# A windowed-attention and routed-MoE kernel: score matmuls in tiles of 32 columns, both masks of a unit together, and loads paced by matmuls

## The chip, the cores and the metric

The kernel runs on one core of a Trainium2 chip. The core has a matmul engine (TensorE; PE in the profile, its weight loads PEld), a vector engine (VectorE, DVE), a scalar engine (ScalarE, ACT), a third engine for elementwise work and gathers (GpSimd, POOL) and a sequencer (SyncE, SP) that here only issues DMAs. Matmul results go to PSUM, which has eight banks of 128 partitions by 512 fp32 numbers; everything else lives in SBUF. The metric is the time of one execution in device microseconds, as the median of several runs.

## The reference

The computation has two stages. The first is attention for 8 batches of 8 heads with head size 64, over 512 local tokens, each of which sees the local tokens at a distance of at most 32 and all 32 global tokens; the 32 global tokens see everything. The second sends each token through one expert of 8 (two matmuls with a relu between them), where the expert is chosen by a scan over the sequence that keeps the previous choice unless a gate is under one half.

```python
k_all, v_all = concat([k_g, k_l]), concat([v_g, v_l])
out_g = softmax(q_g @ k_all.T / 8) @ v_all
s_ll  = where(abs(i - j) <= 32, q_l @ k_l.T / 8, -1e9)
out_l = softmax(concat([q_l @ k_g.T / 8, s_ll])) @ v_all
x = concat([out_g, out_l]) as (batch, 544, 512)
logits = x @ w_gate; local_gate = sigmoid(x @ w_local)
e[s] = argmax(logits[s]) if s == 0 or local_gate[s] < 0.5 else e[s-1]
out[s] = softmax(logits[s])[e] * (relu(x[s] @ w1[e]) @ w2[e])
```

The inputs are random; `q_g` is eight times larger than the rest.

## The kernel before

**Units and steps.** Attention runs over 48 units in an order written out by hand in `Attn.run`: for each batch `l0 l1 g0 l2 g1 l3`. An `l` unit holds the local queries of one pair of heads, a `g` unit the global queries of two pairs. Step s starts unit s and finishes unit s-2, so that every engine always has two units in hand. Each engine takes its instructions in the order in which the program issues them, and semaphores hold an instruction until its inputs are there and its output buffer is free.

**An `l` unit.** `prep` has POOL copy the queries into `qbd` (a block-diagonal layout: 128 contraction rows, 16 windows, 2 heads, 32 queries, where the other head's 64 rows are zero) and the keys into `kx`, one unit ahead and with two buffers of each (L191, L193). For each half of the unit, `l_s` takes a PSUM bank, writes the additive mask into the window's first and last 32 columns with one bf16 matmul against an identity (L238), and adds the scores with eight matmuls, one for each window: 64 columns of weights (both heads of a window) against 128 keys (L243). The contraction spans 128 rows. `l_max` has DVE take the row maximum and the difference (L248, L250), and `l_exp` has ACT take the exponential (L254). Two steps later `l_t` transposes the probabilities (L260, eight 128 by 128 transposes) and ACT copies them out (L262), and `l_av` multiplies them with the values: 16 matmuls a half, with 32 columns of weights each, which write the four groups of 32 PSUM partitions in turn (L276); DVE then normalizes into `xa` (L279 to L284).

**A `g` unit.** `g_s` makes four matmuls with 64 columns of weights (L296); its exponentials, transposes (L328) and value matmuls (L339, 32 columns) follow in the same way.

**Pieces between.** `f1` (L352), `f1g` (L359), `f2` (L367), `f2g` (L375) and `f3` (L385, L388) turn a finished batch into router logits. `fpiece` puts at most one of them between the first score half and the first value half of a step, and one before the second value half. `drip` feeds small DVE, ACT and POOL instructions of the routing between the DVE instructions of the attention; `f4` stores a batch's `xa` (1 MB), `xg` and `gx` to memory.

**Loads.** SP issues every load in program order. A load waits only for its buffer to be free: four buffers `raw` for queries and keys, five `v` for values. At an `l` step the program issues the queries and keys of the pair two ahead and the values of the pair one ahead (1,040 KB in one DMA), so that SP runs ahead of the other engines until the buffers are full.

**After the attention.** The rest of the kernel is expert matmuls in fp32r (L1256, L1267), whose weights SP loads into the same `raw` buffers and others.

In the profile an fp32 matmul is two records, a transpose and a bf16 matmul one. So a score half is 16 records of L243 behind one of L238 for the mask, a value half 32 records of L276.

## Time and profile before

| what | value |
|---|---|
| median of three runs | 690.67 us (690.36 to 690.69) |
| the profiled execution's own time | 694.06 us |
| span of its instructions | 692.3 us |
| attention, to the first expert matmul | about 232 us of the span |
| PE busy in the whole span | 97% |
| DVE, ACT, POOL busy | 62%, 50%, 30% |
| DMA queues, mean rate | 219 GB/s |

The profiler takes one execution. A row of the timeline gives the start in microseconds, the time to the end of the last of the records that it merges, the engine, the line of the program, the operation with the tiles that it writes and reads, rows by columns of the weights, the shape, and the number of records; what stands in brackets is idle time of the engine before it and what ended it. Matmuls overlap, so the time that a group takes is read from its start to the next group's start, not from its own length.

### The profile page before, as it was taken

What the parts mean: (1) busy time and instruction counts of PE and PEld (TensorE: products, weight loads), DVE (VectorE), ACT (ScalarE), POOL (GpSimd) and SP (SyncE); (2) the same over time, 40 slices, a digit from 0 to 9 for tenths busy, and PEclk for the clock granted to TensorE, in tenths of its full rate; (3) what the DMA queues carried; (4) which work ended last, traced back from release to release, by engine and by line L of the source; (5) the groups of instructions that cost most, each with busy time, mean ns of one, the idle gap of its engine ahead of it and who ended that gap; (6) DMA issues with size and microseconds to landing.
All of it is one profiled execution on the core that took longest, in us unless ns stands there. A gap on an engine that the chain in (4) does not pass through costs nothing.

```text
span 692.3 us, 18408 instructions
## 1 busy us (share of the span) xinstructions
PE 670.5 (97%) x7253; PEld 561.1 (81%) x7253; DVE 426.2 (62%) x1050; ACT 342.9 (50%) x614; POOL 207.7 (30%) x342
## 2 busy tenths in 40 slices
PE   9999999999989899998998999999999999999995
PEld 7777777777767787897887988889898889888994
DVE  7878677688887777995517535335354516255572
ACT  4555556555455674653326625344444325255553
POOL 7634334343674301033013303040404020133023
PEclk9999999999999999999999999999999999999999
DMA  8956957866856497777418647337475417265673
GB/s 318 405 220 233 346 193 309 310 248 231 299 196 273 147 356 243 260 243 245 174 60 308 232 149 239 102 117 235 145 225 191 140 61 231 66 222 193 212 270 103
DMA packets 43011, 151.44 MB, mean 219 GB/s; under 512 B 7965, under 2 KB 9245, under 8 KB 38688
## 3 DMA queue, kind: packets, MB, share of 16 engines
q1 hardware_dynamic: 35536, 126.92, 51.6%
q0 software_dynamic: 6960, 21.90, 9.5%
q8 instruction: 77, 1.26, 0.7%
q14 instruction: 150, 1.23, 0.6%
q10 hardware_dynamic: 288, 0.13, 0.1%
HBM read 130.55 MB, written 19.69 MB: 217 GB/s over the span
## 4 chain that ended last, share of the span: by engine, by line
PE 60%; DVE 3%; issue 1%; ACT 0%; POOL 0%; POOLq 0%; DVEq 0%; ACTq 0%
PE ps L1267 29%; PE ps L1256 27%; PE ps L1210 3%; DVE wq L1165 1%; DVE wp L1165 1%; PE ps L1004 0%; PE ps L1379 0%; DVE xl L1165 0%; DVE xT L994 0%; POOL xa L1196 0%; DVE xT L996 0%; POOLq L1427 0%; DVE wp L1213 0%; PE ps L276 0%; DVE wq L1371 0%
## 5 line engine op out<-in xcount | busy, mean ns | idle before, releaser
L1273 POOL DMA_INDIRECT out_dram<-y,tk x39 | 40.4, 1036 | 317.6 <-ACT y L1272 246.3
L1267 PE MATMUL ps<-wp,wq 128*128 128x512 f32 x504 | 128.4, 402 | 1.0 <-ACT wq L1370 1.0
L1267 PEld LDWEIGHTS ps<-wp,wq 128*128 128x128 f32 x504 | 93.5, 190 | 21.1 <-ACT wq L1370 1.2
L1256 PE MATMUL ps<-wp,wp 128*128 128x256 f32 (+5 forms) x672 | 109.3, 322 | 0.2 <-issue 0.2
L1256 PEld LDWEIGHTS ps<-wp,wp 128*128 128x128 f32 x672 | 103.6, 188 | 5.3 <-issue 0.4
L1259 DVE SCALAR_TENSOR_TENSOR wq<-ps,wq 128x256 fp32r<-128x256 f32 (+5 forms) x80 | 41.7, 525 | 72.8 <-ACT wq L1258 62.6
L1213 DVE TENSOR_TENSOR wp<-ps,wp 128x512 fp32r<-128x512 f32 x40 | 27.5, 691 | 78.9 <-ACT wp L1212 78.8
L1258 ACT ACTIVATE wq<-ps 128x256 fp32r<-128x256 f32 (+5 forms) x80 | 37.3, 468 | 78.3 <-PE ps L1256 68.8
L191 POOL TENSOR_SCALAR_AFFINE_SELECT qbd<-raw 64x512 f32<-64x512 f32 x62 | 44.4, 716 | 103.3 <-PE ps L243 85.5
L243 PE MATMUL ps<-kx,qbd 128*64 128x128 f32 x1024 | 71.3, 280 | 0.2 <-issue 0.2
L1272 ACT ACTIVATE y<-ps,pp 128x512 f32<-128x512 f32 x39 | 26.9, 690 | 77.7 <-PE ps L1267 71.1
L243 PEld LDWEIGHTS ps<-kx,qbd 128*64 128x64 f32 x1024 | 55.1, 137 | 12.2 <-issue 7.8
L248 DVE TENSOR_REDUCE mx<-ps 128x4 f32<-128x512 f32 x64 | 43.9, 687 | 29.9 <-PE ps L243 29.9
L1165 DVE TENSOR_TENSOR wp<-raw,wp 128x1024 fp32r<-128x1024 f32 x47 | 57.0, 1217 | 2.8 <-ACT wp L1155 2.8
L254 ACT ACTIVATE pe<-pe 128x512 f32<-128x512 f32 x64 | 40.7, 637 | 31.7 <-DVE pe L250 31.7
L1196 POOL DMA_INDIRECT xa<-xs,idx x42 | 50.9, 1212 | 17.1 <-issue 9.4
L1155 ACT CAST wp<-raw 128x1024 fp32r<-128x1024 f32 x49 | 50.8, 1047 | 0.8 <-ACT hh L1258 0.5
L1212 ACT CAST wp<-ps 128x512 fp32r<-128x512 f32 x40 | 23.4, 590 | 53.9 <-PE ps L1210 53.3
L250 DVE TENSOR_TENSOR pe<-ps,mx 128x512 f32<-128x512 f32 x64 | 44.0, 688 | 1.6
L276 PEld LDWEIGHTS ps<-v,pt 128*32 128x32 f32 x2048 | 33.4, 110 | 13.1 <-issue 7.3
L276 PE MATMUL ps<-v,pt 128*32 128x65 f32 x2048 | 42.8, 222 | 1.1 <-issue 0.4
L262 ACT COPY pt<-ps 128x512 f32<-128x512 f32 x64 | 34.9, 610 | 17.6 <-PE ps L260 17.6
(280 smaller groups left out, 1183.3 us busy)
## 6 DMA issues: line engine op xcount, KB each, us to landing
raw<-in_w_dram SPq DMA_DIRECT2D x78, 512.0 KB, 4.1
v<-in_vw_dram SPq DMA_DIRECT2D x32, 1040.0 KB, 9.8
raw<-in_qk_dram SPq DMA_DIRECT2D x32, 528.0 KB, 8.2
xa<-in_w_dram SPq DMA_DIRECT2D x26, 512.0 KB, 5.2
xT<-in_w_dram SPq DMA_DIRECT2D x20, 512.0 KB, 3.5
xs<-xa SPq DMA_DIRECT2D x8, 1056.0 KB, 4.9
qgb<-in_qg_dram SPq DMA_DIRECT2D x8, 128.0 KB, 3.5
xa<-xs,idx POOLq DMA_INDIRECT x42
```

Source lines behind the costliest of these rows:

```text
L191: self.nc.gpsimd.affine_select(out=out, in_=in_, pattern=pat, compare_op=ALU.is_ge, fill=0.0, base=0, channel_multiplier=0)
L243: nc.tensor.matmul(sp[64 * t2:64 * t2 + 64, t], qbd[:, w], kf[:, f:f + P], start=False, stop=True, skip_group_check=True)
L248: nc.vector.tensor_reduce(out=mx, in_=st["sp"], axis=AX.X, op=ALU.max)
L250: nc.vector.tensor_tensor(out=st["pe"][:, 4 * hb:4 * hb + 4], in0=st["sp"], in1=mx.broadcast_to([P, 4, P]), op=ALU.subtract)
L254: self.nc.scalar.activation(out=pe, in_=pe, func=AF.Exp, scale=SCALE)
L276: nc.tensor.matmul(o[32 * w4:32 * w4 + 32, g, h], pt[:, 2 * g + w4 // 2, w4 % 2, h, :], v[:, w, h * (D + 1):(h + 1) * (D + 1)], start=True ...
L1155: nc.scalar.copy(out=hi, in_=raw)
L1165: (nc.gpsimd if pool else nc.vector).tensor_tensor(out=lo, in0=raw, in1=hi.bitcast(F32), op=ALU.subtract)
L1196: self.nc.gpsimd.indirect_dma_start(out=self.xr[j] if k == "early" else self.xr4[:, j], out_offset=None, in_=src, in_offset=bass.IndirectO ...
L1256: nc.tensor.matmul(ph, a[:, dc, fs], b_[:, dc, n0:n1], start=(n == 0), stop=(n == 11))
L1259: nc.vector.scalar_tensor_tensor(out=hl[:, fc, n0:n1], in0=ph, scalar=0.0, in1=hh[:, fc, n0:n1].bitcast(F32), op0=ALU.max, op1=ALU.subtract)
L1267: nc.tensor.matmul(py, a[:, fc, js], b_[:, fs], start=(fc == 0 and k == 0), stop=(fc == 7 and k == 2))
```

## The change

- `l_s` and `g_s` issue two matmuls with 32 columns of weights (one head each) where one with 64 columns stood. The contraction stays at 128 rows, so that the number of score matmuls doubles and each has half the columns.
- A new `l_m` takes both PSUM banks of an `l` unit and writes both masks right behind the transposes at the start of the step. The second mask stood between the first value half and the second score half.
- Loads are issued by a new `feed`, once in the middle of a step and once at its end. `get` makes each of them wait for the matmul last issued in the program at that place (`gate`). Values come in two DMAs of 520 KB, and queries and keys of the next batch come at the steps k = 3 and k = 5 of a batch of six.
- The store of `xa` is two DMAs in place of one.

The order of PE around the step of an `l2` unit, before. `ps_66` and `ps_63` are the banks of its two score halves, `v_136` belongs to the value halves of unit s-2, L260 are that unit's transposes, and L367 and L385/L388 are pieces.

```order
L260 MATMUL ps_67<-idf,pe_137 128x128 x4
L260 MATMUL ps_68<-idf,pe_137 128x128 x4
L238 LDWEIGHTS idb
L238 MATMUL ps_66<-mask,idb 128x4x2x32
L243 MATMUL ps_66<-kx_146,qbd_144 64x128 x8
L367 MATMUL ps_70<-xT,wgl 32x512 x4
L276 MATMUL ps_69<-v_136,pt_142 32x65 x16
L238 LDWEIGHTS idb
L238 MATMUL ps_63<-mask,idb 128x4x2x32
L243 MATMUL ps_63<-kx_146,qbd_144 64x128 x8
L385 MATMUL ps_64<-idf,gsb 128x128 x4
L276 MATMUL ps_69<-v_136,pt_143 32x65 x16
```

The same place of PE with the change (transposes L289, masks L259, scores L272, `f2` L398, values L305, `f3` L416):

```order
L289 MATMUL ps_67<-idf,pe_137 128x128 x4
L289 MATMUL ps_68<-idf,pe_137 128x128 x4
L259 LDWEIGHTS idb
L259 MATMUL ps_66<-mask,idb 128x4x2x32
L259 LDWEIGHTS idb
L259 MATMUL ps_63<-mask,idb 128x4x2x32
L272 MATMUL ps_66<-kx_146,qbd_144 32x128 x16
L398 MATMUL ps_70<-xT,wgl 32x512 x4
L305 MATMUL ps_69<-v_136,pt_142 32x65 x16
L272 MATMUL ps_63<-kx_146,qbd_144 32x128 x16
L416 MATMUL ps_64<-idf,gsb 128x128 x4
L305 MATMUL ps_69<-v_136,pt_143 32x65 x16
```

The second mask has moved up past a score half, a piece and a value half, and the shape of the score matmuls is 32x128, 16 to a half, where it was 64x128, 8 to a half.

The order of SP's queue for the loads of the third batch, before (`raw` are queries and keys, `qgb` global queries, `v` values):

```order
L178 DMA raw_77<-in_qk_dram 128x1056
L182 DMA qgb_152<-in_qg_dram 128x256
L188 DMA v_134<-in_vw_dram 128x2080
L178 DMA raw_78<-in_qk_dram 128x1056
L188 DMA v_135<-in_vw_dram 128x2080
L178 DMA raw_79<-in_qk_dram 128x1056
L188 DMA v_136<-in_vw_dram 128x2080
```

and with the change, around the same loads, where PE's semaphore is among what each load but that of `qgb` waits for:

```order
L174 DMA v_134<-in_vw_dram 128x1040 x2
L174 DMA raw_77<-in_qk_dram 128x1056
L174 DMA qgb_152<-in_qg_dram 128x256
L174 DMA raw_78<-in_qk_dram 128x1056
L174 DMA v_135<-in_vw_dram 128x1040 x2
L174 DMA raw_79<-in_qk_dram 128x1056
L174 DMA raw_80<-in_qk_dram 128x1056
L174 DMA v_136<-in_vw_dram 128x1040 x2
```

`raw_79` and `raw_80` now stand ahead of `v_136`, and each value tile comes in two loads.

The diff, cut where a hunk only follows from another:

```diff
 
+    def get(self, out, in_):
+        d = self.nc.sync.dma_start(out, in_)
+        if self.gate is not None:
+            self.tc.add_manual_dep(d.ins, self.gate.ins.name, mybir.DependencyInfo(mybir.DependencyClass.Sync, mybir.DependencyReason.DATA), reason="pace")
+
     def load(self, b, pr):
-        nc = self.nc
         if pr == 0:
...
         t = c[("qk", pr)] = self.ld()
-        nc.sync.dma_start(t, self.qk[b, pr])
+        self.get(t, self.qk[b, pr])
 
...
         g = self.cur[b]["qg"] = self.qgb()
-        self.nc.sync.dma_start(g, self.qg[b])
-
-    def loadv(self, b, pr):
-        nc = self.nc
-        v = self.v()
-        self.cur[b]["v"].append(v)
-        nc.sync.dma_start(v.rearrange("p w c -> p (w c)"), self.vw[b, pr])
+        self.get(g, self.qg[b])
+
+    def loadv(self, b, pr, hf):
+        vs = self.cur[b]["v"]
+        if hf == 0:
+            vs.append(self.v())
+        n = NW // 2 * VW
+        self.get(vs[pr].rearrange("p w c -> p (w c)")[:, n * hf:n * hf + n], self.vw[b, pr][:, n * hf:n * hf + n])
+
+    def feed(self, s, hf):
+        b, k = divmod(s, 6)
+        if k < 3:
+            if b == 0 and k < 2 and hf == 0:
+                self.load(0, 2 + k)
+            self.loadv(b, 1 + k, hf)
+            return
+        b += 1
+        if b == B:
+            return
+        if k == 4:
+            self.loadv(b, 0, hf)
+        else:
+            self.load(b, (k - 3) + hf)
+            if (k, hf) == (3, 0):
+                self.load_g(b)
 
...
 
+    def l_m(self, st):
+        nc = self.nc
+        b, pr = st["u"]
+        if pr == 0:
+            self.cur[b]["xa"] = self.xa()
+            self.cur[b]["xg"] = self.xg()
+        st["pe"] = self.pe()
+        st["sps"] = [self.bank(self.ps_s) for _ in range(2)]
+        for hb, sp in enumerate(st["sps"]):
+            mo = sp.rearrange("p t (k c) -> p t k c", c=32)[:, :, 0::3, :]
+            nc.tensor.matmul(mo, self.cst.idb, self.mask[:, 4 * hb:4 * hb + 4], start=True, stop=False, skip_group_check=True)
+
     def l_s(self, st, hb):
         nc = self.nc
-        if hb == 0:
-            b, pr = st["u"]
-            if pr == 0:
-                self.cur[b]["xa"] = self.xa()
-                self.cur[b]["xg"] = self.xg()
-            st["pe"] = self.pe()
         qbd = st["qbd"]
         kf = st["kx"].rearrange("p m c k -> p (m c k)")
-        sp = st["sp"] = self.bank(self.ps_s)
-        mo = sp.rearrange("p t (k c) -> p t k c", c=32)[:, :, 0::3, :]
-        nc.tensor.matmul(mo, self.cst.idb, self.mask[:, 4 * hb:4 * hb + 4], start=True, stop=False, skip_group_check=True)
+        sp = st["sp"] = st["sps"][hb]
         for t in range(4):
...
                 f = 32 * (3 * (w // 2) + w % 2)
-                nc.tensor.matmul(sp[64 * t2:64 * t2 + 64, t], qbd[:, w], kf[:, f:f + P], start=False, stop=True, skip_group_check=True)
+                for h in range(2):
+                    r = 64 * t2 + 32 * h
+                    self.gate = nc.tensor.matmul(sp[r:r + 32, t], qbd[:, w, h], kf[:, f:f + P], start=False, stop=True, skip_group_check=True)
 
...
                     w = 8 * hb + 4 * g + w4
-                    nc.tensor.matmul(o[32 * w4:32 * w4 + 32, g, h], pt[:, 2 * g + w4 // 2, w4 % 2, h, :],
+                    self.gate = nc.tensor.matmul(o[32 * w4:32 * w4 + 32, g, h], pt[:, 2 * g + w4 // 2, w4 % 2, h, :],
                                      v[:, w, h * (D + 1):(h + 1) * (D + 1)], start=True, stop=True, skip_group_check=True)
...
                 k = c[("qk", pr)][:, SL:]
-                nc.tensor.matmul(sp[64 * i:64 * i + 64, 0:n1 - n0], c["qg"][:, pr], k[:, n0:n1], start=True, stop=True, skip_group_check=True)
+                for h in range(2):
+                    r = 64 * i + 32 * h
+                    self.gate = nc.tensor.matmul(sp[r:r + 32, 0:n1 - n0], c["qg"][:, pr, h], k[:, n0:n1], start=True, stop=True, skip_group_check=True)
             st["sp"].append(sp[:, 0:n1 - n0])
...
                 pr, h = 2 * pp + i // 2, i % 2
-                nc.tensor.matmul(op[32 * i:32 * i + 32, 0:D + 1], st["pt"][:, ci, 32 * i:32 * i + 32],
+                self.gate = nc.tensor.matmul(op[32 * i:32 * i + 32, 0:D + 1], st["pt"][:, ci, 32 * i:32 * i + 32],
                                  c["v"][pr][:, w, h * (D + 1):(h + 1) * (D + 1)], start=(ci == 0), stop=(ci == 5), skip_group_check=True)
...
         r0 = P * (1 + col(b))
-        nc.sync.dma_start(self.xs[r0:r0 + 4 * P].rearrange("(t p) r -> p t r", p=P), xa)
+        for t in range(0, 4, 2):
+            nc.sync.dma_start(self.xs[r0 + t * P:r0 + t * P + 2 * P].rearrange("(t p) r -> p t r", p=P), xa[:, t:t + 2])
         r0 = P * (1 + gcol(hf)) + 32 * b4
...
         self.load_g(0)
-        self.loadv(*pairs[0]["u"])
+        for hf in range(2):
+            self.loadv(0, 0, hf)
         self.cst.ident()
...
             if nl:
-                if npr + 2 < len(pairs):
-                    b, i = pairs[npr + 2]["u"]
-                    self.load(b, i)
-                    if i == 0:
-                        self.load_g(b)
-                if npr + 1 < len(pairs):
-                    self.loadv(*pairs[npr + 1]["u"])
                 npr += 1
...
             if nl:
+                self.l_m(nx)
                 self.l_s(nx, 0)
...
                 self.g_max(nx)
+            self.feed(s, 0)
             fpiece()
...
                 self.g_av(st)
+            self.feed(s, 1)
             if nl:
```

More of the change, by code (lines that the diff above doesn't have):

```diff
@@ L134, in __init__ @@
         self.npr = 0
+        self.gate = None
     def make_mask(self):
```

## Prediction

> **What bounds the kernel now.** I read the page first, then busy time by stretches of one batch each, then what PE waited for, then PE's timeline inside a step.
>
> ```profile
> PE 670.5 (97%) x7253; PEld 561.1 (81%) x7253; DVE 426.2 (62%) x1050; ACT 342.9 (50%) x614; POOL 207.7 (30%) x342
> ```
>
> ```profile
> 56.71:85.17 28.46, 28.05 (x588) 21.28 (x587) 21.75 (x77) 16.01 (x38) 11.67 (x27) 1.00 0.75 275
> 85.17:112.81 27.64, 27.64 (x589) 21.20 (x588) 20.55 (x69) 16.01 (x38) 10.46 (x23) 1.00 0.72 268
> 112.81:140.59 27.78, 27.78 (x589) 21.17 (x588) 21.14 (x73) 16.01 (x38) 11.06 (x25) 1.00 0.79 289
> ...
> 168.87:201.51 32.64, 30.83 (x615) 23.09 (x614) 27.41 (x97) 16.00 (x38) 23.24 (x46) 1.00 0.67 239
> 201.51:231.59 30.08, 29.06 (x610) 22.32 (x609) 23.21 (x77) 17.07 (x38) 12.42 (x22) 1.00 0.71 264
> ```
>
> The columns are the stretch, its length, busy time of PE, PEld, DVE, ACT and POOL, the clock, the share of the DMA engines and GB/s. A batch takes 27.7 us and PE is busy for all of it; DVE is at 74 to 76%, ACT at 58%, the DMA engines at 0.72 to 0.79. In the last two stretches, where the routing runs beside, DVE is at 84% and 77%, and PE idles 1.8 and 1.0 us.
>
> ```profile
> PE ps L276 <- issue: 0.4, 1, 0.4
> PE ps L243 <- issue: 0.2, 1, 0.2
> ```
>
> These are all of PE's waits from 28 to 160 us (engine and line, what ended the wait, us in total, times, longest): 0.6 us, none of it for a load. So attention is bound by PE. But "busy" holds something that is no streaming, and the timeline shows it:
>
> ```profile
> 107.31 1.09 PE L260 MATMUL ps<-idf,pe 128*128 128x128 f32 x8
> 108.24 0.27 PE L238 MATMUL ps<-mask,idb 128*128 128x256 bf16 x1
> 108.44 1.09 PE L243 MATMUL ps<-kx,qbd 128*64 128x128 f32 x16
> 109.46 0.67 PE L276 MATMUL ps<-v,pt 128*32 128x65 f32 x32
> 110.06 0.28 PE L238 MATMUL ps<-mask,idb 128*128 128x256 bf16 x1
> 110.27 1.09 PE L243 MATMUL ps<-kx,qbd 128*64 128x128 f32 x16
> 111.30 0.67 PE L276 MATMUL ps<-v,pt 128*32 128x65 f32 x32
> ```
>
> Start to start, a score half (128*64: 128 rows, 64 columns of weights) takes 1.02 us, a value half 0.60, a mask 0.20. Compare groups that are followed by one of the same width:
>
> ```profile
> 66.30 1.14 PE L296 MATMUL ps<-raw,qgb 128*64 128x256 f32 x8
> 67.36 0.27 PE L375 MATMUL ps<-xgT,wgg 128*32 128x32 f32 x8
> 67.45 0.64 PE L276 MATMUL ps<-v,pt 128*32 128x65 f32 x32
> ...
> 71.36 1.07 PE L367 MATMUL ps<-xT,wgl 128*32 128x512 f32 x8
> 72.24 0.64 PE L276 MATMUL ps<-v,pt 128*32 128x65 f32 x32
> ```
>
> L367 has 32 columns of weights, four matmuls side by side: 8 records of 512 columns are 2 x 512 = 1,024 column times and take 0.88 us to the next 32-column group. A score half is 16 records of 128 columns, two side by side, also 1,024 column times, and takes 1.02 to the next group, which is of another width. The difference, 0.14 us, is what a change of width costs. The value half gives the same: 32 records of 65 columns, four side by side, are 520 column times, 0.45 us at L367's pace, and it takes 0.60 before a mask: 0.15. L375, 8 records with 32 columns each, hands over to L276 in 0.09. I take 0.145 us for a change of width.
>
> **The change part by part.**
>
> *Score matmuls in 32 columns.* There are 64 score halves:
>
> ```profile
> L243 PE MATMUL ps<-kx,qbd 128*64 128x128 f32 x1024 | 71.3, 280 | 0.2 <-issue 0.2
> L238 PE MATMUL ps<-mask,idb 128*128 128x256 bf16 x64 | 17.8, 279 | 0.0
> ```
>
> Each becomes 32 records of 128 columns, four side by side: again 1,024 column times. No row has just this shape, but it lies between L276 (65 columns: 0.60 - 0.145 = 0.455 us for 32 records) and L367 (512 columns: 0.11 us a record), and both go at the same 0.86 to 0.88 ns a column time. So the arithmetic costs as before, and what is won is the width. For the records that are added the rows allow two ends: nothing, or the whole of the present 55 ns a record (0.88 / 16) if that is a price per record and not per column. L276's 14 ns a record (0.455 / 32) says that it is per column, and I take nothing.
>
> I counted neighbours in PE's order, before and with the change. Of the 64 score halves, 38 are now followed by a 32-column group (values, `f2`, or the second score half); before, each was followed by a change of width. Of the value halves, 23 were followed by a mask and are now followed by scores. Of the `g` units' scores, 8 are now followed by `f2g` or values. Against that, 7 pieces `f1` that were followed by a mask of their own width are now followed by scores. 38 + 23 + 8 - 7 = 62 changes of width fewer, at 0.145: 9.0 us. If neighbours of one width cost the wait too, it is 0; if a change of width costs the 0.17 us that PEld idles before such a group, 10.5:
>
> ```profile
> 111.30 0.50 PEld L276 LDWEIGHTS ps<-v,pt 128*32 128x32 f32 x32 [0.17 <-issue]
> ```
>
> *Both masks behind the transposes.* A mask before scores takes 0.20 us. The first of a pair is now followed by one of its own shape. The nearest row is that of expert matmuls with 256 columns and full width, in the chain that ended last:
>
> ```profile
> 638.13 11.34 PE ps L1256 x96
> ```
>
> 0.118 us each. So 32 masks cost 0.118 in place of 0.20: 2.7 us. The ends: 0, if the identity has to be loaded anew between the two and PE waits for it, and 4.6, if the whole 0.145 goes; L1256 loads new weights for every matmul, so I keep 2.7. The second bank must be free some 2 us earlier; there are four banks, an `l` unit takes two, and its predecessor but one has been read by then, since DVE takes each half up at once and has 24% to spare. Cost nothing; without that cover, PE would wait for L250, 0.69 us.
>
> Together PE has 11.7 us less to do.
>
> *Loads behind matmuls.* SP issued loads as early as buffers allowed, in bursts, and they landed late but long before use:
>
> ```profile
> v<-in_vw_dram SPq DMA_DIRECT2D x32, 1040.0 KB, 9.8
> raw<-in_qk_dram SPq DMA_DIRECT2D x32, 528.0 KB, 8.2
> ```
>
> (KB each and median us from issue to landing.) Now each waits for a matmul, one portion in a half step, 0.53 MB in 2.3 us. The tightest is the first pair of the next batch: issued behind the first score half at k = 3, copied by POOL, used by the first scores at k = 0. Before, these two were here:
>
> ```profile
> 98.65 1.09 PE L243 MATMUL ps<-kx,qbd 128*64 128x128 f32 x16
> ...
> 112.81 1.09 PE L243 MATMUL ps<-kx,qbd 128*64 128x128 f32 x16
> ```
>
> ```profile
> 111.45 1.50 POOL L191 TENSOR_SCALAR_AFFINE_SELECT qbd<-raw 64x512 f32<-64x512 f32 x2 [6.04 <-PE ps L243]
> 113.02 1.33 POOL L191 TENSOR_SCALAR_AFFINE_SELECT kx<-raw 128x128 f32<-128x128 f32 x4
> ```
>
> 14.2 us from the one to the other; less 1.0 for the matmul, 2.9 for the copies, and some 0.8 that the step shrinks, 9.5 us are left for a landing that took 8.2 with up to 3 MB in flight. With one portion in flight it will be shorter. Values are issued three steps ahead. Behind a waiting load in SP's queue stand the next loads and the stores of `xa`, `xg` and `gx`, whose buffers are needed again two batches later; and behind those stores the second half of one value tile, needed two steps later:
>
> ```profile
> 119.55 0.38 SPq L413 DMA_DIRECT2D xs<-xa  x1
> 119.98 3.60 SPq L417 DMA_DIRECT2D xs<-xg  x4
> ```
>
> They take SP 4 us of a batch, and the second DMA for `xa` adds another 0.4, under those two steps of 9 us. So the pacing costs nothing, and since PE waited for no load, it wins nothing.
>
> *Who is late next.* DVE. A half costs it 0.69 (L248) + 0.69 (L250) + 0.16 + 0.18 + 0.42 (L279 to L284) = 2.14 us:
>
> ```profile
> 109.58 0.69 DVE L248 TENSOR_REDUCE mx<-ps 128x4 f32<-128x512 f32 x1 [1.43 <-PE ps L243]
> ...
> 110.31 0.69 DVE L250 TENSOR_TENSOR pe<-ps,mx 128x512 f32<-128x512 f32 x1
> 110.92 0.15 DVE L279 TENSOR_SCALAR rs<-ps 128x4 f32<-128x4 f32 x1
> ...
> 111.10 0.18 DVE L281 RECIPROCAL rs<-rs 128x4 f32<-128x4 f32 x1
> ...
> 111.32 0.42 DVE L284 TENSOR_TENSOR xa<-ps,rs 128x256 f32<-128x256 f32 x1
> ```
>
> Over a batch its 21 us still fit into 27.7 - 1.4 = 26.3 (80%). In the two routing batches it rises to some 27.4 of 31.2 (88%) and 23.2 of 28.6 (81%), where PE waits already; I let half of their two times 1.4 us be lost, 1.4 us, and 0.4 in the first two steps, which wait for copies and not for PE. 11.7 - 1.8 = 9.9 us.
>
> The profiled execution took 694.06 us around a span of 692.3, 0.5% above the median of 690.67. 9.9 us less is 684.2 there and **680.8 us** as a median. The expert stage is the same code and starts as much earlier.
>
> **The rivals.**
>
> *B, DVE takes half.* Within a unit, two score halves now follow each other after 1.33 us (0.88 + 0.45) in place of 1.83, and DVE has 2.14 us for each. If the backlog reaches the next unit's value halves, whose two banks DVE must empty, half of PE's 11.7 us comes back as waits on L284, beside the 0.4 at the start: 685.2, up to 688. For it, such waits are there in the routing batches (PE's waits from 160 to 232 us):
>
> ```profile
> PE ps L352 <- DVE xa L284: 1.0, 2, 0.6
> PE ps L276 <- DVE xa L284: 0.4, 1, 0.4
> ```
>
> Against: pieces, transposes and `g` units let DVE catch up, and it idles 24%.
>
> *C, loads come late (the other side).* If a landing takes longer than those 9.5 us, PE waits for POOL's copies in each of 7 batches. At 11 us it costs 1.5 x 7 = 10.5 us, which eats the gain; that is the point from which the kernel is slower. At 13 us, 24.5 us: 705. For it: the medians of 8.2 and 9.8 are near. Against: they come from bursts.
>
> *D, a price per record.* The score and `g` matmuls double. If a record costs 55 ns whatever its columns, a score half takes 1.76 us: 64 x 0.88 = 56, and 690.7 + 56 - 11.7 = 735. It is slower than before from 33 ns on (0.88 + 11.7 / 64 = 1.06, over 32). L276's 14 ns speak against it. [...]
>
> *E, the waits stay.* If PE also empties itself between 32-column scores, which add to a bank, and 32-column values, only the masks gain: 688. Against it, L367 hands over in 0.88, and L339, which adds to its bank too, goes at L276's pace:
>
> ```profile
> 106.49 0.89 PE L339 MATMUL ps<-v,ptg 128*32 128x65 f32 x48
> ```
>
> (0.82 us to the transposes at 107.31, less 0.145, over 48: 14 ns a record).
>
> **How the numbers follow.** A 0.60, B 0.22, C 0.05, D 0.03, E 0.05, and 0.05 for B and E together, which ends at no change. A by itself lies between 677.5 (10.5 + 2.7 and nothing lost) and 683. The range goes from 677 to 686.5: it takes in A and most of B, 0.8 in all. A measurement of this kernel tells 0.2% (1.4 us) from no change. Faster: A, B and E, 0.87; same 0.05; slower, C and D, 0.08.
>
> **What would show it.** In the new profile a score half before a value half should take 0.86 to 0.90 us start to start, a value half before scores 0.45, the first mask 0.12, and a batch 26.3 us with PE busy throughout. Waits of PE on L284's successor say B; waits on POOL's copies, with POOL waiting for a load of `raw`, say C; score halves over 1.0 us say D if their records are spread evenly, E if the gap is at the end. What would make it wrong above all is DVE's lateness, which I priced by a share and not by a chain.

## The result and the profile after

The changed kernel takes 713.42 us (median of four runs, 712.40 to 714.97) beside 690.68 for the kernel before in the same session: a ratio of 1.033 (95% interval 1.0305 to 1.0354). It is slower, by 22.7 us, where 680.8 was forecast. The profiled span is 710.8 us. The first expert matmul starts at 249.5 us where it started at 231.6, and what follows takes 461.3 us as against 460.7: the loss lies in the attention.

The page of the changed kernel, busy time of the whole span:

```profile
PE 667.8 (94%) x8405; PEld 563.7 (79%) x8405; DVE 424.7 (60%) x1050; ACT 344.3 (48%) x614; POOL 209.2 (29%) x342
```

PE has 1,152 records more and is busy for 2.7 us less, in a span that is 18.5 us longer. The stretches of one batch each (the columns are as in the prediction: stretch, length, busy time of PE, PEld, DVE, ACT, POOL, clock, DMA share, GB/s):

```profile
30.44:57.05 26.61, 26.38 (x733) 21.16 (x732) 21.26 (x81) 16.05 (x38) 11.07 (x25) 1.00 0.82 253
57.05:91.51 34.46, 28.73 (x732) 22.28 (x731) 20.86 (x73) 16.20 (x38) 11.06 (x25) 0.90 0.73 222
91.51:125.56 34.05, 29.75 (x733) 22.64 (x732) 21.91 (x74) 16.49 (x39) 11.91 (x27) 0.90 0.73 235
125.56:156.84 31.28, 27.79 (x732) 21.79 (x731) 20.21 (x72) 16.00 (x38) 10.27 (x23) 0.95 0.78 242
156.84:188.12 31.28, 26.95 (x733) 20.80 (x732) 22.38 (x82) 16.48 (x39) 11.07 (x25) 1.00 0.79 254
```

The first of these batches takes 26.6 us: the 26.3 of the prediction came true here. From the next one on a batch takes 31 to 34, and the clock falls below 1.00. PE inside an undisturbed step (L259 masks, L272 scores, L305 values):

```profile
87.38 0.38 PE L259 MATMUL ps<-mask,idb 128*128 128x256 bf16 x2
87.69 1.08 PE L272 MATMUL ps<-kx,qbd 128*32 128x128 f32 x32
88.59 0.64 PE L305 MATMUL ps<-v,pt 128*32 128x65 f32 x32
89.05 1.06 PE L272 MATMUL ps<-kx,qbd 128*32 128x128 f32 x32
89.92 0.64 PE L305 MATMUL ps<-v,pt 128*32 128x65 f32 x32
```

A score half takes 0.90 and 0.87 us start to start, a value half before scores 0.46, the pair of masks 0.31 (0.12 + 0.20 was forecast). PE's work got shorter as foreseen. What takes the time stands in the waits from 28 to 250 us (engine and line, what ended the wait, us in total, times, longest):

```profile
DVE xa L313 <- DMA xs<-xa: 26.4, 8, 7.6
...
PE ps L398 <- DVE xa L313: 13.3, 4, 5.0
...
PE ps L383 <- DVE xa L313: 3.7, 6, 1.2
```

DVE waits for the store of `xa`, and PE for DVE. Here is the first time. SP's queue:

```profile
58.19 9.95 SPq L174 DMA_DIRECT2D v<-in_vw_dram  x5
68.23 0.90 SPq L445 DMA_DIRECT2D xs<-xa  x2
```

DVE:

```profile
64.20 0.08 DVE L800 MEMSET xa<- 128x28 f32 x1
...
69.07 0.18 DVE L310 RECIPROCAL rs<-rs 128x4 f32<-128x4 f32 x1
76.82 0.42 DVE L313 TENSOR_TENSOR xa<-ps,rs 128x256 f32<-128x256 f32 x1 [7.57 <-DMA xs<-xa]
```

PE:

```profile
71.18 1.08 PE L272 MATMUL ps<-kx,qbd 128*32 128x128 f32 x32
77.30 1.94 PE L398 MATMUL ps<-xT,wgl 128*32 128x512 f32 x8 [5.04 <-DVE xa L313]
79.01 1.09 PE L305 MATMUL ps<-v,pt 128*32 128x65 f32 x32
```

The tile of batch 0 is complete at 64.3 us, its store is issued at 68.2, since the fifth value load ahead of it in SP's queue waits for a matmul, and lands at 76.8. There are two `xa` buffers, and the first value half of batch 2 has to be written into this one at 69.3. The kernel before, at the same place (SP, then DVE):

```profile
63.46 0.38 SPq L413 DMA_DIRECT2D xs<-xa  x1
```

```profile
63.35 0.08 DVE L771 MEMSET xa<- 128x28 f32 x1
...
68.63 0.42 DVE L284 TENSOR_TENSOR xa<-ps,rs 128x256 f32<-128x256 f32 x1
```

It issued the store as soon as the tile was complete, and 5.2 us later, little more than the median landing time of 4.9 us, the buffer was written again. That reuse had no time to spare, and I had not looked at it. With the change the store is late twice over: at the four stalls it is issued 3.9 to 4.6 us after the tile is complete, and its first half then takes another 5.2 to 8.5 us to land.

The stall costs twice. Windows of the changed kernel behind it:

```profile
75.00:76.00 1.00, 0.00 (x0) 0.00 (x0) 0.00 (x0) 0.00 (x0) 0.00 (x0) 0.50 0.31 86
...
80.00:81.00 1.00, 1.00 (x28) 0.92 (x24) 0.76 (x3) 0.63 (x1) 0.00 (x0) 0.50 0.77 283
81.00:82.00 1.00, 1.00 (x20) 0.72 (x12) 0.31 (x2) 0.00 (x0) 0.32 (x1) 0.89 0.03 10
```

The granted clock is 0.50 for 6.8 us from the middle of the stall, and L398 above takes 1.71 us to the next group where 0.88 was its pace. The attention has three such stretches (6.8, 6.8 and 3.4 us), the kernel before none. The first begins at 74.4 us, when PE has stood for 2.1 us of a stall of 5.0; the other two begin at 108.5 and 142.7 us, inside stalls of 2.7 and 3.3 us. Two more stalls, of 2.6 us up to 21.5 and of 2.3 us up to 174.4, have none.

So that kernels can be compared, each is split in the same way: the end of the attention, less all waits of PE up to there, less half of the time that PE worked at half clock. The rest is what PE had to do.

```
kernel            end    PE waits  of these:            half   rest
                  of     in all    for     behind xa    clock
                  att.             nothing              loss
before            231.6     5.1      0.8      1.4        0.0   226.5
after             249.5    26.7      4.5     17.3        6.4   216.4
```

The rest fell by 10.1 us; waits rose by 21.6 and half clock by 6.4. "Nothing" are waits that the profile names "issue": nothing that it shows was missing.

### The profile page after: what moved, and what is told of

Read it like the earlier page. It is cut to its first block, busy times and chain, and to the rows that moved or that the text cites. A ratio compares the mean times of both kernels' runs of the same rounds, so it can differ in the third digit from the quotient of the medians.

```text
span 710.8 us, 20840 instructions
## 1 busy us (share of the span) xinstructions
PE 667.8 (94%) x8405; PEld 563.7 (79%) x8405; DVE 424.7 (60%) x1050; ACT 344.3 (48%) x614; POOL 209.2 (29%) x342
## 4 chain that ended last, share of the span: by engine, by line
PE 54%; DVE 6%; issue 1%; ACT 1%; POOL 0%; POOLq 0%; DVEq 0%; ACTq 0%
PE ps L1296 26%; PE ps L1285 24%; PE ps L1239 2%; DVE wp L1194 2%; DVE wq L1194 1%; DVE hl L1288 1%; PE ps L1408 1%; DVE xT L1023 0%; DVE xT L1025 0%; POOL xa L1225 0%; DVE o L939 0%; DVE xl L1242 0%; PE ps L1033 0%; POOLq L1456 0%; DVE wp L1242 0%
## 5 line engine op out<-in xcount | busy, mean ns | idle before, releaser
L272 PE MATMUL ps<-kx,qbd 128*32 128x128 f32 x2048 | 70.6, 280 | 0.2 <-POOL kx L214 0.2
L272 PEld LDWEIGHTS ps<-kx,qbd 128*32 128x32 f32 x2048 | 54.7, 112 | 8.7 <-issue 6.0
L1225 POOL DMA_INDIRECT xa<-xs,idx x42 | 51.5, 1226 | 17.3 <-issue 9.7
L305 PE MATMUL ps<-v,pt 128*32 128x65 f32 x2048 | 44.8, 226 | 5.7 <-issue 3.8
L305 PEld LDWEIGHTS ps<-v,pt 128*32 128x32 f32 x2048 | 36.6, 113 | 17.0 <-issue 11.6
L214 POOL TENSOR_SCALAR_AFFINE_SELECT kx<-raw 128x384 f32<-128x384 f32 (+3 forms) x127 | 42.7, 369 | 2.7 <-DMA raw<-in_qk_dram 0.6
```

The source lines that it names most:

```text
L214: self.nc.gpsimd.affine_select(out=out, in_=in_, pattern=pat, compare_op=ALU.is_ge, fill=0.0, base=0, channel_multiplier=0)
L272: self.gate = nc.tensor.matmul(sp[r:r + 32, t], qbd[:, w, h], kf[:, f:f + P], start=False, stop=True, skip_group_check=True)
L305: self.gate = nc.tensor.matmul(o[32 * w4:32 * w4 + 32, g, h], pt[:, 2 * g + w4 // 2, w4 % 2, h, :], v[:, w, h * (D + 1):(h + 1) * (D + 1)] ...
L1225: self.nc.gpsimd.indirect_dma_start(out=self.xr[j] if k == "early" else self.xr4[:, j], out_offset=None, in_=src, in_offset=bass.IndirectO ...
```

## The experiments

The expectations name theories by letters. S: the store of `xa` is late behind gated loads. T: the narrow matmuls themselves cost more. H: the halved portions and the new order of the loads cost. Later I: PE gets its instructions late. A, B, C and D are the prediction's; Q, W, N and R are said where they come. Runs of one session are compared with the kernel before on the same chip.

**e1_tiles: the matmuls alone.** The kernel before with 32-column scores and both masks together; loads and stores as before.

```diff
+                for h in range(2):
+                    r = 64 * t2 + 32 * h
+                    nc.tensor.matmul(sp[r:r + 32, t], qbd[:, w, h], kf[:, f:f + P], ...)
```

> The score tiles of 32 columns and the two masks together, with the loads and stores as they were before. Theory S (a store of xa stands behind a load that waits for a matmul, DVE waits for the store, PE for DVE): nothing of that is here, and PE has 11.7 us less to do, so 679 to 684 us. Rival T (the new tiles themselves cost time): above 691.

**e2_paced: the loads alone.** The changed kernel with the old `l_s` and `g_s` (64 columns, second mask in its old place).

> The loads behind matmuls in half portions and the store in two, with PE's work as before. Theory S: all of the loss is here, 713 and the 11.7 us that PE has more to do, some 720 to 726 us. Rival T: at most 700.

**e3_no_gate: no load waits for a matmul.** The changed kernel, with its order of loads, portions and split store.

```diff
-        if self.gate is not None:
+        if False:
             self.tc.add_manual_dep(...)
```

> The changed kernel without the wait of a load for a matmul; order, halves and the two-part store stay. Theory S: the store gets past the loads as soon as their buffers are free, and the time is that of the tiles alone, 679 to 686 us. Rival H (half portions and the new order are what makes the stores late): above 700.

**e4_store_act: stores from ACT's queue.** In `f4` of the changed kernel every `nc.sync.dma_start` becomes `nc.scalar.dma_start`.

> The changed kernel with the stores of xa, xg and gx issued by ACT in place of SP, so that no load stands ahead of them; every load still waits for its matmul. Theory S: the 26 us in which DVE waited for stores go to under 5, and the time to 684 to 692 us (the first steps stay late by 2 to 3 us). Rival C (loads for POOL's copies come late): above 704.

Measured, in one session (before 692.2):

```
kernel         us     ratio (95%)             end of att.  for nothing  behind xa  half clock  rest
e1_tiles      706.7   1.019 (1.012 to 1.026)     244.7        17.2         2.9        3.3      217.4
e2_paced      715.2   1.033 (1.028 to 1.038)     252.8         0.3        14.7        9.9      223.8
e3_no_gate    709.3   1.022 (1.017 to 1.028)     249.4        19.3         3.0        4.9      218.8
e4_store_act  738.0   1.067 (1.061 to 1.072)     262.5         1.9         2.7       13.2      216.4
```

The matmuls (with the masks) and the loads each lose by themselves. e2 shows the stall without any change of PE's work, though its time lies below the 720 to 726 expected; its waits of DVE, then of PE:

```profile
DVE xa L307 <- DMA xs<-xa: 27.1, 8, 6.2
```

```profile
PE ps L390 <- DVE xa L307: 13.6, 4, 3.9
```

and in e3, with the gate gone, the wait is gone with it:

```profile
DVE xa L313 <- DMA xs<-xa: 0.9, 2, 0.6
```

So the gate, and not the portions, makes the store late: that much of S is shown. Whether the store is late by its place in the queue or by what is in flight while it lands, e3 can't tell; e4 and e8 can. With the portions and the new order e3 is about where e1 is, so H is out, though the time is above 700 as H had it. But e1 and e3 are slow too, and e1 has none of the new loads. PE's work is short in it (217.4), so T is out as well, and PE waits 17.2 us for nothing that the profile shows:

```profile
PE ps L249 <- issue: 5.7, 3, 2.6
PE ps L304 <- issue: 3.6, 3, 2.2
PE ps L347 <- issue: 2.9, 4, 1.1
```

These waits stand inside or between groups whose inputs are there (e1's timeline; L336 transposes, L304 the scores of a `g` unit), while the DMA engines are full (e1's windows):

```profile
51.55 0.88 PE L336 MATMUL ps<-idf,pg 128*128 128x128 f32 x6
54.61 1.12 PE L304 MATMUL ps<-raw,qgb 128*32 128x256 f32 x16 [2.18 <-issue]
```

```profile
50.00:52.00 2.00, 2.00 (x58) 1.54 (x50) 1.86 (x6) 0.43 (x1) 1.43 (x2) 1.00 0.97 386
52.00:54.00 2.00, 0.43 (x4) 0.30 (x3) 1.21 (x7) 1.39 (x3) 1.33 (x4) 1.00 1.02 411
```

That is a second mechanism, which none of my theories had. e4 missed: issuing the seven stores of a batch keeps ACT's queue, the first time from 66.5 to 73.7 us, and ACT's copies stand behind them, a wait that the profile puts down to the store that landed last (ACT's waits, then PE's):

```profile
ACT xT L384 <- DMA xs<-xa: 22.3, 4, 6.4
```

```profile
PE ps L289 <- ACT xT L384: 15.3, 6, 4.4
```

And DVE goes on waiting for the store, with no load ahead of it in its queue; under 5 us were expected:

```profile
DVE xa L313 <- DMA xs<-xa: 22.0, 8, 4.6
```

So the time is above 704, as C had it, but not for C's reason.

**Theory I.** The page counts transfers of an instruction queue (transfers, MB, share). Before and after:

```profile
q8 instruction: 77, 1.26, 0.7%
```

```profile
q8 instruction: 87, 1.43, 0.9%
```

1.26 MB over 77 are 16 KB each. Up to 260 us PE of the kernel before executes 4,897 matmul and 4,898 weight-load records over 38 transfers: 258 for each. So I take a transfer for 256 instructions of PE, an estimate from these counts. The densest stretch is two score and two value halves, 256 records in the changed kernel: 0.90 + 0.46 + 0.87 + 0.46 = 2.7 us. Before, 256 records of scores, values and masks took some 4.8 us (196 in 2 x 1.82). For every kernel I took how many records PE had executed when a transfer began, less 256 for each transfer ahead of it. If the estimate holds, that number can't pass what PE had in store:

```
kernel           transfers in   us for   greatest  number   waits for nothing
                 the attention  each     number    >= 410   of 0.4 us or more
before               36          6.43      400        0       1,  0.4 us
e5_masks             36          6.36      398        0       1,  0.4
e19_xa3_64_ord       36          6.40      407        0       3,  2.3
e20_xa3_half_ord     41          5.67      421        2       5,  5.3
e13_second32         41          5.83      449        3       9, 10.4
e10_split            44          5.60      440        3       7,  7.6
e11_less_dma         45          5.16      436        1       7,  6.0
after                45          5.54      449        1       2,  3.2
e1_tiles             45          5.44      449        7      12, 16.6
e18_xa3_ord          45          5.34      449        5      10, 12.9
```

In four of these the greatest number is 449, and in none more. In e1, 447, 445, 449 and 446 are reached by the transfers at 30.1, 52.0, 150.0 and 230.6 us, and PE's four longest waits end 2.3 to 2.6 us after these. I read this as PE running dry there, and the late transfers are those that begin under full DMA engines: in e1 the 15 that begin with 350 records or more have the engines at 1.00 in the 2 us ahead of them (0.92 to 1.06), the 17 that begin with under 260 at 0.35. At 256 for each, 449 is less than two transfers bring; what sets it no view shows.

**e5_masks and e10_split: does the number of records do it?** e5 is the kernel before with `l_m` and 64-column scores. e10 is the kernel before with each window's score matmul cut along its moving columns:

```diff
-                nc.tensor.matmul(sp[64 * t2:64 * t2 + 64, t], qbd[:, w], kf[:, f:f + P], ...)
+                for n in range(0, P, 64):
+                    nc.tensor.matmul(sp[64 * t2:64 * t2 + 64, t, n:n + 64], qbd[:, w], kf[:, f + n:f + n + 64], ...)
```

> The kernel before with both masks of a unit behind the transposes, nothing else: the same number of records on PE. Theory I (the waits for nothing that PE shows in the 32-column kernel come from the doubled number of its instructions, whose refill is late): no such waits here (under 2 us), and the masks' 32 x 0.085 = 2.7 us are won: 687 to 689.5. Rival W (the waits come from the moved masks, that is from the order): 5 us or more of such waits, and 692 or more.

> The kernel before with every score matmul of the windows split into two of 64 moving columns with the same weights, still 64 columns wide: 1,024 more records on PE, no arithmetic more, no change of width more or less, loads as before. Theory I (the number of instructions and their refill): 8 us or more of waits for nothing on PE, a score half as before 1.02 us where it isn't cut by one, 699 to 712. Rival T (the waits belong to matmuls that are 32 columns wide): under 3 us of such waits, 690 to 693. Rival D (a price for each record): no waits for nothing, but a score half of 1.2 to 1.5 us, evenly, 702 to 720.

**e8_store_first and e9_first_qk: the store not behind gated loads.**

```diff
-            self.loadv(b, 1 + k, hf)
+            if k == 0:
+                self.loadv(b, 1, hf)
+            elif hf == k - 1:
+                self.loadv(b, 1 + k, 0)
+                self.loadv(b, 1 + k, 1)
```

> The changed kernel with one thing moved: in the third step of a batch no value load stands ahead of the stores in SP's queue any more (the two halves for the second step are issued together behind that step's scores, the two for the third together at its end); all loads still wait for a matmul. Theory S (the loss of the changed kernel is the store of xa, late behind gated loads): DVE's waits for the store of xa fall from 26.4 to under 5 us, PE's waits behind DVE's write of xa from 17.3 to under 4, the stretches of half clock after them go too (three of 6.8, 6.8 and 3.4 us, worth some 8 us), attention ends at 222 to 229 instead of 249.5, and the time is 684 to 694, since PE's 11.7 us are then left less some 2 at the start and 4 of waits for nothing. Rival Q (the store is late because evenly spread loads keep the DMA engines full while it lands, wherever it stands in SP's queue): over 12 us of waits for the store remain, 700 to 712.

> As e8_store_first, and q and k of the first batch's third and fourth pairs are issued at the start without waiting for a matmul. Theory of the start (the changed kernel begins its seventh step 2.2 us later because POOL waits 7.5 us for these tiles up to there): that step starts at 28.3 instead of 30.4, and the time is 2 us below e8_store_first: 682 to 692. Rival (the start is bound by POOL's and ACT's copies all the same): within 0.7 us of e8_store_first.

Measured, in one session (before 692.4):

```
kernel           us     ratio (95%)               end of att.  for nothing  behind xa  half clock  rest
e5_masks        690.6   0.9967 (0.9947 to 0.9988)    228.8         0.9         1.5        0.0      222.7
e10_split       707.6   1.022 (1.018 to 1.026)       246.5         8.1         0.8        1.7      233.4
e8_store_first  705.7   1.021 (1.015 to 1.026)       239.8        11.8         3.5        3.3      216.3
e9_first_qk     704.3   1.018 (1.013 to 1.023)       241.7        13.5         2.8        3.2      218.7
```

e5's attention ends 2.75 us earlier, as expected, with no more waits for nothing than before; by the medians it gains 1.8 us, a little less than expected. It is the only version here that beats the kernel before. e10 has the old width and the old loads, 1,024 matmul records more, and the waits are there (between the value half at 108.34 and L329):

```profile
111.05 0.87 PE L329 MATMUL ps<-idf,pg 128*128 128x128 f32 x6 [2.09 <-issue]
```

with the DMA engines at 0.96 and 1.04 around it. So a larger number of instructions brings the waits without the 32 columns and without the new order of the masks, and W is out. With nearly the same number e1 has twice as much of them; its records also go by faster. e10 also prices a record: the score half, which was expected to stay as it was, takes 1.12 us in place of 1.02, that is some 6.5 ns for each of 16 added records, 6.7 us in all, about the growth of its rest (6.9).

```profile
84.77 1.20 PE L244 MATMUL ps<-kx,qbd 128*64 128x64 f32 x32
85.89 0.67 PE L277 MATMUL ps<-v,pt 128*32 128x65 f32 x32
```

e8 took the stall from PE (17.3 to 3.5 us) and the attention ends 9.7 earlier, but DVE's waits for the store only fell from 26.4 to 15.8. In e8 the store is issued 0.2 us after the tile is complete (66.3 us) and still lands late (SP, then DVE):

```profile
66.46 1.19 SPq L449 DMA_DIRECT2D xs<-xa  x2
```

```profile
74.10 0.42 DVE L317 TENSOR_TENSOR xa<-ps,rs 128x256 f32<-128x256 f32 x1 [2.01 <-DMA xs<-xa]
```

Value loads are in flight ahead of it. In the 6 us from the issue of a store of batches 0 to 3 the DMA engines are at 0.92 to 0.96 in e8 and at 0.84 to 0.90 in the changed kernel, as against 0.56 to 0.66 before and 0.57 to 0.58 in e3. So Q's numbers came true (over 12 us of waits, 700 to 712): the store is late both by its place in the queue and by what is in flight while it lands, and both come with the gate. Of S's numbers only those for PE came true. The waits for nothing rose from 4.5 to 11.8; I read this as PE's instructions having caught up, in the changed kernel, while PE stood. e9 missed: it lies 1.4 us below e8, between its two expectations. The seventh step starts at 28.7 us in both, so the start was not a matter of those loads; the changed kernel's longest wait for nothing, 2.6 us, ends at 21.5 us.

**e11_less_dma, e12_masks_g, e13_second32: the two sides of a late transfer.** e11 is e1 without the value loads of batches 1 to 7. Its routing comes out otherwise (the whole takes 733.9 us), so that only its attention is compared. e12 and e13 add 32-column scores to e5 in two doses.

```diff
+        if b > 0:
+            self.cur[b]["v"].append(self.v0[pr])
+            return
```

> e1_tiles (32-column scores, both masks together, loads as before) with the value loads of batches 1 to 7 left out: they use the values of batch 0, and 29 MB less are loaded. Theory I with full DMA engines (PE's instructions are transferred late because the engines are full of loads): waits of PE for nothing fall from 17.2 to under 2 us, attention ends at 218 to 223, and the time is 676 to 682, that is, the predicted gain of PE shows once the loads are out of the way. Rival N (PE can't be supplied with so many instructions in any case): 8 us or more of such waits, 690 or more.

> e5_masks and 32-column scores for the global units alone: 64 records more on PE. If a change of width costs 0.145 us, 8 of them go: 1.2 us less than e5_masks, less 64 x 6.5 ns for the records: 686 to 690, waits for nothing under 2 us. If the refill of instructions is at its edge already: 2 us or more of such waits, and no gain.

> e12_masks_g and 32-column scores for the second half of each unit's windows: half of the added records, and about two thirds of the changes of width saved (some 45 x 0.145 = 6.5 us against e12_masks_g). If late instructions cost in proportion to the records (16.4 us for 1,088 in e1_tiles, so 8 to 9 for 576): 690 to 694. If there is a threshold, since packets may be late as long as PE has instructions: under 4 us of waits for nothing, 681 to 687, the best version so far.

Measured, in one session (before 695.4):

```
kernel          us     ratio (95%)               end of att.  for nothing  behind xa  half clock  rest
e11_less_dma     -      -                           232.4         6.6         4.0        0.0      217.5
e12_masks_g    695.1   0.9991 (0.9977 to 1.0005)    231.6         2.8         1.3        0.0      224.3
e13_second32   703.0   1.011 (1.009 to 1.013)       238.9        12.1         2.3        0.0      220.5
```

Windows from 30 to 180 us, of e1 and of e11:

```profile
30.00:180.00 150.00, 136.75 (x3650) 108.89 (x3650) 105.75 (x376) 80.18 (x185) 54.31 (x119) 0.98 0.66 243
```

```profile
30.00:180.00 150.00, 144.20 (x3950) 115.46 (x3952) 117.77 (x408) 86.12 (x196) 59.70 (x131) 1.00 0.35 119
```

With half of the traffic PE gets through 3,950 matmul records in the same time in place of 3,650, and the attention is 12.3 us shorter. Of the 17.2 us of waits 10.6 go with the loads. So full DMA engines are most of what makes the transfers late, and N is out. The expectation was still too good (under 2 us of waits, an end at 218 to 223). Of the 6.6 us left, 2.2 lie in the first 28 us, where the engines are still at 0.87. Of the later waits the two longest, 1.2 and 1.6 us, come with transfers that begin behind 2 us at 0.87 and 0.90, but two of some 0.5 us come behind 0.50 and 0.47. Waits for DVE and ACT cost 3.8 more than before the change. In e12 64 more records bring 2.8 us of waits for nothing in place of e5's 0.9, and no gain, the worse of its two expectations. e13 missed both of its own: half of the records cost 12.1 us, not half of 17.2, so the lateness is not in proportion, and no threshold saves it with the old loads.

**e14 to e17: a third buffer for `xa`, and a fault.** The idea was to keep the pacing and give the store a whole batch more. To make room, the value buffers became four.

```diff
-NV = 5
+NV = 4
-        self.xa = ring(tl, [P, 4, ROW], F32, "xa", 2)
+        self.xa = Ring(ring(tl, [P, 4, ROW], F32, "xa", 2).t + [at1.tile([P, 4, ROW], F32, name="xa2", tag="xa2")])
```

> The changed kernel with a third buffer for xa, so that a buffer is written again three batches later and not two, and with four value buffers in place of five to make room; loads paced one portion a half step as in the changed kernel. Theory S with I (two faults: the store behind gated loads, and PE's instructions late under loads): DVE waits under 2 us for a store, none of the three stretches of half clock, waits of PE for nothing between 4.5 (the changed kernel) and 12 (e8_store_first); attention ends at 225 to 233, 683 to 694. Rival R (whatever stall is removed, the refill takes the same back, since PE without stalls needs its instructions faster): 12 us or more of such waits, attention ends at 236 or later, 697 or more.

> As e14_xa3, and q and k of the first batch's third and fourth pairs are issued at the start. If the 2.2 us that the changed kernel loses before its seventh step come from these loads: 1 to 2.5 us below e14_xa3. If the start is bound by the instructions or the copies: within 1 us of it.

> As e14_xa3, but scores in 64 columns as before the change, that is, pacing, three xa buffers and both masks together. The number of PE's instructions is that of the kernel before: waits for nothing under 1 us (e2_paced had 0.3), no wait for a store, attention ends at 226 to 230, 686 to 690 as e5_masks. Had pacing a cost of its own beside the store (the landing of q and k, the smaller portions), it would end at 232 or later.

> As e14_xa3, but the first half of a unit's windows in 64 columns and only the second half, and the global units, in 32: half of the added records. Theory I with a threshold (packets are late only up to some bound, and paced loads keep them under it): waits for nothing under 4 us, attention ends at 222 to 227, 681 to 687. If lateness costs in proportion to the records even with paced loads: between e14_xa3 and e16_xa3_64, and no better than the better of the two.

They took 742.5, 742.6, 745.1 and 743.9 us (before 695.4) and tell nothing on S or I: with four buffers the first value tile of the next batch was issued ahead of the last reader of the old one, which then waited for it and read the new values in place of the old (PE's waits in e14):

```profile
PE ps L370 <- DMA v<-in_vw_dram: 23.6, 6, 5.9
```

**e18, e19, e20: the same, mended.** Steps k = 4 and k = 5 of `feed` are exchanged.

```diff
-        if k == 4:
+        if k == 5:
             self.loadv(b, 0, hf)
         else:
-            self.load(b, (k - 3) + hf)
+            self.load(b, 2 * (k - 3) + hf)
```

> e14_xa3 mended: there the first value tile of the next batch was written over the one that the global unit still had to read, and PE waited 28 us for it. Now that tile is loaded one step later, and the third and fourth q and k one step earlier. Theory S with I, as for e14_xa3: no wait for a store, no wait for values, attention ends at 225 to 233, waits of PE for nothing 4.5 to 12, 683 to 694. Rival R (the refill takes back what the stall gave): 12 us or more of such waits, attention ends at 236 or later, 697 or more.

> e16_xa3_64 mended in the same way: paced loads, three xa buffers, both masks together, scores in 64 columns. Waits for nothing under 1.5 us, attention ends at 226 to 230, 686 to 690, as e5_masks. If pacing costs something beside the store, 232 or later.

> e17_xa3_half mended in the same way: half of the added records. With a threshold: waits for nothing under 4 us, attention ends at 222 to 227, 681 to 687. In proportion: between e18_xa3_ord and e19_xa3_64_ord.

Measured, in one session (before 692.3):

```
kernel             us     ratio (95%)               end of att.  for nothing  behind xa  half clock  rest
e18_xa3_ord       703.0   1.014 (1.011 to 1.016)       240.5        14.1         3.3        1.7      217.9
e19_xa3_64_ord    692.1   0.9996 (0.9984 to 1.0007)    230.3         2.5         1.3        0.0      222.8
e20_xa3_half_ord  695.9   1.006 (1.004 to 1.008)       232.4         6.0         3.0        0.0      219.5
```

No kernel of the three waits for a store. e19 says that pacing by itself costs little once the store has its buffer: it takes the time of the kernel before, its attention ends 1.3 us before the old one and 1.5 after e5's, with 1.5 us more waits for nothing than e5, and each of its figures lies just above what was expected. e18 answers the question: all of R's numbers came true. Without the store's stall PE runs into waits for nothing, 14.1 us of them, the longest here (e18's timeline and windows):

```profile
73.24 0.40 PE L305 MATMUL ps<-v,pt 128*32 128x65 f32 x12
77.05 0.60 PE L305 MATMUL ps<-v,pt 128*32 128x65 f32 x18 [3.41 <-issue]
```

```profile
72.00:74.00 2.00, 1.64 (x44) 0.88 (x33) 1.33 (x2) 1.03 (x3) 0.00 (x0) 1.00 1.01 398
```

It breaks a value half in the middle, in a stretch in which the DMA engines move 398 GB/s. The doses with paced loads are 2.5, 6.0 and 14.1 us for none, half and all of the added records: here the lateness grows faster than the dose, but half of the records cost 3.5 us already, the threshold that was expected (under 4 us of waits) isn't there, and the best of the three is the one without 32-column scores.

## Why the prediction was wrong

- **What bounds the kernel.** Right: PE bounds the attention, and a change of width costs time: a score half took 1.02 us before values of another width and takes 0.87 to 0.90 before values of its own.
- **The score matmuls and the masks, 11.7 us less for PE.** Right in the mechanism, somewhat too large. The rest of PE's work fell by 3.7 us in e5 and e19 (masks) and by 7.7 to 10.2 in eight kernels with all scores in 32 columns (after, e1, e3, e4, e8, e9, e11, e18; mean 9.1). The split is good to some 3 us: e2, whose work is that of the kernel before, comes out 2.7 lower. The halves have the lengths that were named, 0.87 to 0.90 and 0.46.
- **"For the records that are added ... I take nothing."** This step failed. For PE's streaming it was right in the halves shown (0.87 to 0.90 us, where 0.86 to 0.90 was named); e10, where the same weights are loaded twice, has 6.5 ns a record. But a record is also an instruction: the kernel before has 9,795 records up to 260 us beside 38 transfers of 16 KB in the instruction queue. That queue was on the page, at 0.7% of the 16 DMA engines beside 51.6% for the queue with the loads, and I neither priced nor named it. The waits that I put down to it are 17.2 us in e1, 14.1 in e18, and 4.5 in the changed kernel, where the other fault hides it.
- **"... the stores of `xa`, `xg` and `gx`, whose buffers are needed again two batches later ... So the pacing costs nothing."** This step failed, and it is the larger share of the loss: PE waits 17.3 us behind DVE's `xa`, 13.3 of them right behind DVE's four stalls for the store, and loses 6.4 at half clock. The sentence counts the two batches from the wrong end. A batch is stored while the batch but one after it begins, so that of the two batches some 5 us were left, the landing time of the store. I had the row of the store before me and asked only how long it keeps SP, not how long it stands there behind loads that wait, nor how late it lands among them.
- **DVE is late (B), 1.8 us.** About right: PE's waits behind DVE's `xa`, other than for the store, are 4.0 us in the changed kernel and 2.9 to 4.0 in e1, e3, e11 and e18, as against 1.4 before.
- **C, loads late for POOL's copies.** POOL waited for `raw` for 29.6 us as against 8.5, but PE for POOL only 0.2. The point from which it decides wasn't reached. As the other side, C was the wrong mechanism: I looked at the loads behind the gate and not at what else stands in their queue. The 0.08 for a slower kernel stood for C and D, and neither came; the result was slower by two mechanisms that the prediction didn't have.
- **D and E.** Refuted by the score halves of 0.87 to 0.90 us, as the prediction said they would be.
- **The sum.** By the split above: 231.6 + 21.6 (waits) + 6.4 (half clock) - 10.1 (work) = 249.5, the measured end of the attention. The forecast had +1.8, 0 and -11.7.

What stays open: that a transfer of instructions is late because the DMA engines are full rests on e1 against e11 and on the windows around the waits, and e11 keeps 4.4 us of waits after its first 28 us; how a transfer queues inside an engine no view shows. How much of the store's lateness is its place in the queue and how much its landing is told apart only by e8, in which other loads moved too.

## What to carry to other kernels

When small matmuls are split into smaller ones, count the instructions beside the arithmetic: here 256 of PE's densest records take 2.7 us, e1's four longest waits end 2.3 to 2.6 us after a late transfer of instructions began, behind DMA engines at 1.00, and the profile calls such a wait "issue". Before a load is made to wait, list everything behind it in its queue, and for each store there take from the trace how long before the rewrite of its buffer it lands; "a batch later" is no time. And take the parts of a change one by one: here the 32-column scores and the gated loads each lost alone, and each hid part of the other, while the masks alone gained 1.8 us.

## What was not expected of the hardware

- PE's records ahead of its refill, counted with 256 for each transfer (an estimate), never passed 449 in the ten kernels of the table, and four of them reached that number. A transfer came every 5.2 to 6.4 us.
- Of the changed kernel's five stalls of PE over 2 us in the attention, three (5.0, 2.7 and 3.3 us) came with a granted clock of 0.50, for 6.83, 6.83 and 3.41 us, and two (2.6 and 2.3 us) without. From 80 to 81 us PE has work from end to end at 0.50.
- The first portion of the split store took 8.6 us to land (68.2 to 76.8) while the engines moved up to 387 GB/s (72 to 74 us) for other loads, where the single one took a median of 4.9, with the engines at 0.56 to 0.66 in the 6 us from its issue: in these runs evenly spread loads left no quiet time for the store.
